# An attention and FFN block on Trainium2: the list scheduler in the source is replaced by a written order of all 2,455 operations

## The chip, the cores and the metric

One Trainium2 chip, of which the kernel uses one core. The metric is the device time of one execution in microseconds (us); before the change it is 489.09 us, the median of 3 runs (488.92 to 490.06).

The engines are called as the profile calls them: PE multiplies (TensorE), DVE is VectorE, ACT ScalarE, POOL GpSimd, and SP issues transfers. Each engine works through its own list of instructions in order; semaphores hold an instruction back until what it reads is there and what it overwrites has been read.

## The reference

```python
S, D, H, Dh, F = 2048, 512, 32, 16, 1792
xn  = layernorm(x)                                    # x [S, D], float32
q, k, v = split(xn @ wqkv)                            # 32 heads of 16
phi(u) = [softmax(u @ w_phi), softmax(-(u @ w_phi))]  # per head, 32 features
kv  = phi(k)^T v ;  z = sum_s phi(k)
o   = (phi(q) kv) / (phi(q) z + 1e-6)
s   = o @ wo
g   = silu(mish(xn @ w1 + b1) @ w2)
out = x + s * g
```

## The kernel before

Every float32 product is made of three PE products of a high and a low part (names ending in `h` and `l`: ACT rounds to the high part, and DVE or POOL subtracts it from the source to get the low one). Large products are cut 2 by 2 in the manner of Strassen, seven block products instead of eight, whose sums DVE and ACT form.

The work in order of time: the head loads x and the weights, folds `w_phi` into the weights of q and k (`wqf`, `wkf`, products with `phit`) and normalizes and transposes x (`pt`, 16 token tiles `N0` to `N15`; the transposed blocks are `fh`, `fl`). Then k and v (`kx`, `ky`, `kz`, `kj`) with the sums over tokens (`kvp`), q (8 blocks, banks `qx`, `qy`, `qz`, 256 columns a product), the first FFN product (14 blocks, `fx`, `fy`, `fz`, 512 columns; its result `hd` goes to DRAM), the attention (`ph` are transposed features of q, `pn` the products with kv), the output product (`pw`, its result goes to DRAM as `so`), and last the second FFN product (`y`, 256 columns): for each of 8 token blocks T and 7 pairs b of F chunks, `act(T, b)` loads `r`, applies mish, forms three sums in `r` (two 128x128 operations and one of 128x2x128, which the trace shows as 128x256), rounds to `ah` and subtracts to `al` (128x896), and PE multiplies seven combinations with `w2`. `final` and `gate` apply silu, multiply with `sr` (a load of `so`), add `xx` (a load of x) and store to out.

The functions of `block_kernel` do not emit instructions. They record operations in `Program` (from line 73): an operation is one instruction or a group (the six matmuls of one block product, for instance), with the tiles that it reads and writes. Some can go to either of two engines (`either`: DVE or POOL; `copy` and `held`: ACT or DVE). At the end `issue` (line 397) emits all of them at line 404, which is why most instructions of the trace have that one line; they are told apart by tiles.

What order they are emitted in is decided by `Program.order` (183) and `simulate` (222). The functions are called in the order of the string `ORDER` (parts such as `Ka2`, `Q4`, `G16`), and PE's operations keep this order. For everything else `simulate` is a list scheduler: it steps through a modelled time with the costs of `cost`, models of transfers and of the port that DVE and POOL share, and at each step gives an idle engine the ready operation whose due time (`late`) is first, if its tile buffers are free (`fits`) and nothing more urgent comes within its duration (`better`). The due time of an operation comes from the planned time of PE's next use, with single corrections from the table `SHIFT`. For an operation that two engines can take, whichever is idle first takes it.

`issue` also adds one kind of dependency: a POOL operation waits for the last DVE operation that takes the shared port, if that ends in the modelled time less than `NEAR` = 4000 ns earlier.

Tile buffers come from pools of fixed size (38 large and 15 half-size buffers, 8 PSUM banks among others); a buffer's next user waits for its last reader.

Of the kernel before, what the change touches and what calls it, by code (L numbers as in the profile page):

```python
# [48 lines left out]
SHIFT = """  # L49
kd:0:-9100 wv1:0:-1100 N1:2:-15000 N1:3:300 N1:5:5800 N1:13:4300 N1:14:-7000 kl:3:-10000 Ka2:3:-9700 N5:6:-2200  # L50
N5:8:-1200 N5:11:13000 N2:0:-3500 N2:2:-2000 N3:4:1500 N3:13:-11400 Kc0:7:4900 Kc0:10:14200 k4:0:-6900 Kd0:6:300
N6:14:-6700 P0:1:4800 P0:5:3800 P0:11:5000 Kb1:3:300 N7:6:-2800 N7:8:7300 N7:9:-6400 N8:8:-2700 N9:13:3600 Kc1:8:1800
Kd1:4:-7300 N10:3:-300 N11:0:5800 P4:0:-7000 P4:4:300 P4:5:3100 N14:8:-6800 Kd3:1:-5000 Kd3:6:-6400 A2:0:-3600
N13:5:-2500 Fa4:1:-1100 Fa4:3:3600 N15:4:10800 N15:6:-5000 N15:11:-300 Kc5:6:4400 Ka6:1:-600 Kc6:5:-300 Kc6:6:2600
P6:6:-1100 P6:8:5100 P3:3:-2600 P3:11:-2000 Kb7:1:2800 Fa3:1:-300 Fa3:3:300 P2:4:-2000 P2:6:1100 P2:10:800 Kd6:6:-8800
Kd6:9:-9500 Fb6:3:-2300 Fc3:1:1600 Fc3:2:800 Fc3:4:7900 wQ:1:2300 wQ:13:6600 Fa2:3:300 Fa2:4:-1900 Fa1:3:900
M4:1:-1400 P5:10:3200 Q0:7:14700 Q0:23:-2000 z:4:1200 z:5:11100 D0:0:800 D0:4:4700 D0:8:-800 L:5:-4200 L:9:-3000
D1:2:-8100 Q1:16:800 Q1:19:300 Q2:3:-15000 Q2:9:-2500 Q2:15:300 Q2:25:-1900 Q3:17:-4300 Q3:18:4700 Fc5:5:9400
D3:7:1800 D4:3:-4000 D4:4:6800 D4:5:1300 D4:6:11900 D4:10:11500 D5:1:-300 Fb11:1:-4700 Q4:7:-600 Q4:16:600 Q4:18:7800
Q4:20:800 Q4:21:-1400 Q4:23:-8800 Q5:25:-600 M3:1:-5000 M3:2:-6700 Fa12:1:800 D6:6:-500 D6:10:300 Fb10:1:-500  # L60
D7:1:5000 D7:4:6600 D8:1:-2400 D8:4:-500 D8:10:1400 Q6:1:4700 D9:10:800 Q7:1:7800 Q7:16:-4700 Q7:20:4800 Q7:21:-13000
Q7:23:-12900 M2:2:-5000 D10:6:-800 M6:2:-4100 D11:1:-1700 Ua0:1:-1100 Ua0:12:-800 Fc9:1:3400 D12:5:-5000 D13:0:-4400
D13:4:12500 Fa13:4:800 Ub0:14:-4300 wo0:1:-4500 Fc13:4:-13100 Fc7:2:15000 R0:8:4700 D14:6:-7800 O3:2:-900 Ua1:2:-4200
Ua1:4:-6700 Ua1:6:-3100 Ua1:11:-5000 Ua1:13:-300 Ua1:14:300 O5:2:-500 Fd13:2:-4200 O6:1:-2200 Ub1:5:-5000 Ub1:6:-2000
Ub1:8:-4500 G7:4:-2000 R2:0:-2200 R1:1:15000 R1:6:4200 R1:10:5800 G8:3:-5000 G8:6:1900 O11:2:-2000 R6:1:4900 R3:2:1600
R3:8:-3300 R4:1:2000 G11:0:-6800 G12:5:3100 G12:6:-1200 G13:5:-1100 G32:3:6500 G34:6:4000 G1:4:-15000 G3:0:5000
G4:0:-4100 G5:5:4000 G35:3:9300 G35:4:-5800 G35:6:3100 G14:0:-10200 G14:3:4000 E0:6:-2600 G15:2:800 G39:6:-300
G16:4:-5000 G41:3:1700 E5:4:-300 G20:0:800 G20:2:-2000 G20:3:-5300 G20:6:-5000 G42:3:5100 G42:5:-300 G43:2:4200
G44:2:300 G44:4:-2000 H4:2:1300 G46:3:6600 G46:6:300 G24:6:500 G47:5:-3000 G26:4:-1600 E6:2:-800 G49:0:-5000
G49:2:4000 G49:6:-1100 G49:9:2000 G49:12:-2200 G49:19:2200 G49:26:5000 G49:31:800 G49:36:2800 G49:42:-4700 G49:43:800  # L70
E7:9:-300 E7:10:15000 H3:7:2300 H6:8:800
"""
ACT_SET = {AF.Exp: 1, AF.Silu: 3, AF.Mish: 2}


class Op:
    __slots__ = ("impl", "reads", "writes", "at", "idx", "succ", "ndep", "late", "new", "ready", "start", "eng", "sets", "slack", "open", "soon", "pos", "deps", "lock", "part", "half", "code", "tiles", "shift")


class Program:  # L80


    def __init__(self, nc):
        self.eng = {"PE": nc.tensor, "V": nc.vector, "G": nc.gpsimd, "A": nc.scalar, "Q": nc.sync}
# [3 lines left out]
        self.shifts = {k: int(v) for k, _, v in (c.rpartition(":") for c in SHIFT.split())}

    @staticmethod  # L90
    def cost(e, m, a, k):
        aps = [v for v in a if isinstance(v, bass.AP)]
        n = aps[0].free_size()
        if e == "PE":
            if m == "transpose":
                return 109
            n, c = aps[2].free_size(), aps[1].free_size()
            if aps[1].dtype == F32R:
                return max(n / 2.4 + 0.104 * c, c * 0.835 + 2)
            full = 2 * max(n / 1.2 + 2.5, c * 0.835)  # L100
            if aps[1].shape[0] == 32:
                return max(0.155 * n, 24)
            return max(full * aps[0].shape[0] / P, 27)
        if e == "Q":
            return 450
# [1134 lines left out]
```

## Time and profile before

| | |
|---|---|
| time, median of 3 runs | 489.09 us (488.92 to 490.06) |
| the profiled execution, span from the first to the last instruction | 488.7 us (no other time is given for it) |
| its granted TensorE clock | 1.000 |
| PE busy | 480.2 us, 98% |
| DVE busy | 446.2 us, 91% |
| ACT busy | 293.4 us, 60% |
| POOL busy | 267.2 us, 55% |
| PE waiting after its first product | 2.8 us in 7 waits |

The span is 0.4 us below the median of the runs. A busy PE is not PE at its peak: its matmuls are pipelined, so the duration of one is longer than the interval at which they follow each other (a dense 512-column matmul has 0.39 us and follows the one before after 0.23).

In a row of a timeline the bracket holds the idle time of the engine just before the instruction and what ended it; "x6" is a run of six such instructions, whose duration is that of the run. Rows that group by form leave buffer numbers out.

### The profile page before, as it was taken

Reading aid. Unit: us, or ns where it says so; the run is one execution under the profiler, and the core shown is the slowest. Engines: PE = TensorE matmul, PEld = TensorE weight load, DVE = VectorE, ACT = ScalarE, POOL = GpSimd, SP = SyncE. Lnnn points to the kernel's source line nnn. Section 1 sums busy time; section 2 is a strip of 40 time slices with the busy share of each in tenths; the row PEclk is TensorE's granted clock in tenths of the full one; section 3 lists DMA queues with packets and bytes.
Section 4 is the critical chain, followed back from the end, with each engine's and each line's share of the span. In section 5 each row is a group of like instructions: output and inputs, shape, how many; then the busy total and the mean of one; then the engine's idle time right before and its main releaser. Section 6 shows DMA issues by size and latency. Waiting matters only on the chain.

```text
span 488.7 us, 10325 instructions
## 1 busy us (share of the span) xinstructions
PE 480.2 (98%) x3820; PEld 426.2 (87%) x3820; DVE 446.2 (91%) x893; ACT 293.4 (60%) x453; POOL 267.2 (55%) x197
## 2 busy tenths in 40 slices
PE   8899999999999999999999999999999999999996
PEld 7788888888887889898887878788899999999996
DVE  6999999988899999999999899889989889999894
ACT  3997545654556453635345545677879687777631
POOL 3989998998490446798987686370021024120030
PEclk9999999999999999999999999999999999999999
DMA  8812923968867689982959635726465646578172
GB/s 294 265 48 109 332 99 122 312 197 272 315 217 313 225 301 345 394 300 87 310 199 341 229 115 211 261 85 207 141 193 165 201 154 211 194 234 269 44 250 94
DMA packets 68641, 105.70 MB, mean 216 GB/s; under 512 B 6896, under 2 KB 37744, under 8 KB 68592
## 3 DMA queue, kind: packets, MB, share of 16 engines
q1 hardware_dynamic: 68448, 104.79, 62.9%
q8 instruction: 30, 0.49, 0.4%
q10 hardware_dynamic: 144, 0.26, 0.2%
q14 instruction: 19, 0.16, 0.1%
HBM read 60.60 MB, written 44.43 MB: 215 GB/s over the span
## 4 chain that ended last, share of the span: by engine, by line
PE 81%; DVE 8%; DMA 5%; issue 2%; ACT 1%; SPq 1%; POOL 1%; DVEq 0%; ACTq 0%
PE y L404 20%; PE fx L404 14%; PE pw L404 9%; PE kx L404 7%; PE fy L404 7%; PE qx L404 5%; PE ky L404 3%; PE fz L404 3%; PE qy L404 2%; PE kj L404 2%; PE pn L404 2%; PE kz L404 2%; DVE al L404 2%; DMA wvr<-wv 1%; DMA w1a<-w 1%
## 5 line engine op out<-in xcount | busy, mean ns | idle before, releaser
L404 POOL TENSOR_TENSOR al<-r,ah 128x896 fp32r<-128x896 f32 x8 | 17.0, 2130 | 87.4 <-DMA r<-hd 35.1
L404 ACT ACTIVATE ah<-r 128x896 fp32r<-128x896 f32 x56 | 50.9, 944 | 16.0 <-DVE r L404 12.9
L404 DVE TENSOR_TENSOR al<-r,ah 128x896 fp32r<-128x896 f32 x48 | 54.8, 1171 | 5.0 <-ACT ah L404 3.2
L404 DVE TENSOR_TENSOR r<-r 128x128 f32<-128x128 f32 (+1 forms) x157 | 48.3, 353 | 5.0 <-ACT r L404 3.4
L404 PE MATMUL y<-w2h,al 128*128 128x256 f32 x160 | 45.4, 283 | 0.0
L404 PE MATMUL y<-w2h,ah 128*128 128x256 f32 x160 | 45.3, 283 | 0.0
L404 PE MATMUL y<-w2l,ah 128*128 128x256 f32 x160 | 45.3, 283 | 0.0
L404 PE MATMUL y<-w2t,ah 128*128 128x256 f32 x224 | 41.0, 283 | 0.0
L404 PE MATMUL fx<-fh,w1b 128*128 128x512 f32 x112 | 38.8, 393 | 0.0
L404 ACT ACTIVATE r<-r 128x512 f32<-128x512 f32 x56 | 33.2, 621 | 7.9 <-DMA r<-hd 7.9
L404 PEld LDWEIGHTS y<-w2t,ah 128*128 128x128 f32 x224 | 34.9, 192 | 0.0
L404 PE MATMUL y<-w2t,al 128*128 128x256 f32 x112 | 31.7, 283 | 0.0
L404 PEld LDWEIGHTS y<-w2h,al 128*128 128x128 f32 x160 | 30.7, 192 | 0.6 <-issue 0.4
L404 PEld LDWEIGHTS y<-w2l,ah 128*128 128x128 f32 x160 | 30.7, 192 | 0.2
L404 PEld LDWEIGHTS y<-w2h,ah 128*128 128x128 f32 x160 | 30.7, 192 | 0.0
L404 PE MATMUL y<-w2g,ah 128*128 128x256 f32 x160 | 30.4, 283 | 0.0
L404 PEld LDWEIGHTS fx<-fh,w1b 128*128 128x128 f32 x112 | 21.0, 188 | 5.4 <-issue 1.2
L404 PEld LDWEIGHTS y<-w2g,ah 128*128 128x128 f32 x160 | 25.0, 192 | 0.0
L404 POOL TENSOR_TENSOR r<-r 128x128 f32<-128x128 f32 (+1 forms) x11 | 6.4, 592 | 32.3 <-DMA sr<-so 22.5
L404 PE MATMUL y<-w2g,al 128*128 128x256 f32 x80 | 22.6, 283 | 0.0
L404 ACT ACT_TABLE_LOAD x13 | 16.7, 1283 | 9.2 <-DMA x<-x 4.1
L404 PE MATMUL fx<-fl,w1b 128*128 128x512 f32 x56 | 21.8, 390 | 0.0
(766 smaller groups left out, 1730.0 us busy)
## 6 DMA issues: line engine op xcount, KB each, us to landing
r<-hd SPq DMA_DIRECT2D x56, 256.0 KB, 3.5
xd<-xc SPq DMA_DIRECT2D x8, 896.0 KB, 4.1
w1b<-w1d SPq DMA_DIRECT2D x14, 512.0 KB, 5.5
w1b<-w1d SPq DMA_DIRECT2D x14, 384.0 KB, 4.9
so<-so SPq DMA_DIRECT2D x16, 256.0 KB, 2.1
x<-x SPq DMA_DIRECT2D x15, 256.0 KB, 3.7
w1a<-w SPq DMA_DIRECT2D x7, 512.0 KB, 4.6
...
```

The costliest lines, as they stand in the source:

```text
L404: ins = getattr(e, m)(*a, **k)
```

## The change

`simulate` and all that serves it alone (the constants `PEN` to `BEGIN`, `SLACK`, `AHEAD`, `LAT`, `SHIFT`, `ACT_SET`, `cost`, `records`, `halves`, `links`, `volume`, `reads`, `bcast`, and the calls of `halves`) go. In their place stands `PLAN`, a string of 2,455 names: `Ka2.0` is the first operation that part `Ka2` records, and a last letter V, G or A gives the engine of an operation that two engines can take. `order` puts the operations in that order. Now PE's operations stand in an order of their own too, no longer in that of `ORDER`. What is computed, in which groups and with which tiles, is as before. `NEAR` is now counted in places of the plan.

```diff
-WAKE, EACH, NEAR = 15, 2, 4000
+WAKE, EACH, NEAR = 15, 2, 24
...
-SHIFT = """
-kd:0:-9100 wv1:0:-1100 N1:2:-15000 N1:3:300 N1:5:5800 N1:13:4300 N1:14:-7000 kl:3:-10000 Ka2:3:-9700 N5:6:-2200
...
+PLAN = """
+@.0 @.1 @.2 @.3 @.4 N1.0 N4.0 @.15 N4.3 @.17 N0.0 N1.1 N1.2 wv0.0 N1.3 N4.1 N4.2 @.16G N1.4 @.5 @.6 @.7 @.8 @.9 @.10
...
     def order(self):
+        at = {o.name: o for o in self.ops}
+        plan = []
+        for c in PLAN.split():
+            e = c[-1] if c[-1] in self.eng else ""
+            o = at.pop(c[:-1] if e else c)
+            o.eng = e or next(iter(o.impl))
+            plan.append(o)
+        assert not at
...
+        return plan
...
     def issue(self, tc):
         first, held = True, None
-        for o in self.order():
-            for i, (m, a, k) in enumerate(o.impl[o.eng][1]):
+        for n, o in enumerate(self.order()):
+            for i, (m, a, k) in enumerate(o.impl[o.eng]):
...
-                if i == 0 and o.eng == "G" and held is not None and o.start - held[1] < NEAR:
+                if i == 0 and o.eng == "G" and m != "dma_start" and held is not None and n - held[1] < NEAR:
...
-                held = ins.ins.name, o.start + o.impl["V"][0]
+                held = ins.ins.name, n
```

Between the first and the second left-out piece of `order` the new code also checks that the writers and readers of each tile keep the order in which the functions recorded them.

Three places of the lists of instructions. The first is PE in the head, before (the end of the first kz product, the folds `wqf` of the first pair of q weights, and the next k product `kj00`):

```order
L404 MATMUL kz2_188<-wv1l_161,fh10_105 128x512
L404 MATMUL kz2_188<-wv1h_160,fh10_105 128x512
L404 MATMUL wqf21_192<-phit_101,wqT10_190 128x128 x4
L404 MATMUL wqf31_193<-phit_101,wqT10_190 128x128 x4
L404 MATMUL kj00_194<-wv0h_142,fl00_104 128x512
L404 MATMUL kj00_194<-wv0l_143,fh00_103 128x512
L404 MATMUL kj00_194<-wv0h_142,fh00_103 128x512
L404 MATMUL kj00_194<-wv0h_142,fl00_104 128x512
L404 MATMUL kj00_194<-wv0l_143,fh00_103 128x512
```

and now, first around `wqf21`:

```order
L256 MATMUL kx2_187<-wv0l_143,fh00_103 128x512
L256 MATMUL kx2_187<-wv0h_142,fh00_103 128x512
L256 MATMUL wqf21_192<-phit_101,wqT10_190 128x128 x4
L256 MATMUL kz2_188<-wv1h_160,fl10_106 128x512
L256 MATMUL kz2_188<-wv1l_161,fh10_105 128x512
```

Behind these rows follow four more of `kz2`, the twelve of `kj00` and six of a later k product, `kj03`. The last three of those, and what now stands behind them:

```order
L256 MATMUL kj03_215<-wkh0_144,xl0_176 128x512
L256 MATMUL kj03_215<-wkl0_145,xh0_175 128x512
L256 MATMUL kj03_215<-wkh0_144,xh0_175 128x512
L256 MATMUL wqf31_193<-phit_101,wqT10_190 128x128 x4
L256 MATMUL pt2_207<-ident_83,x2_202 128x128 x4
```

`wqf31` stood directly behind `wqf21`; now 24 matmuls stand between them, and `wqf21` stands ahead of kz instead of behind it. The transposes of tile 5 (`pt5`), not shown, have moved from behind the last `wkf` fold to two folds earlier.

The second is PE in q block 4, whose last product into bank `qx4` reads `wq1`; before (the end of a product into `qx4`, one into `qy4`, and the start of the next into `qx4`):

```order
L404 MATMUL qx4_661<-wqs1h_493,fh51_589 128x256
L404 MATMUL qy4_663<-wqs1h_493,fl21_584 128x256
L404 MATMUL qy4_663<-wqs1l_494,fh21_583 128x256
L404 MATMUL qy4_663<-wqs1h_493,fh21_583 128x256
L404 MATMUL qy4_663<-wqs1h_493,fl21_584 128x256
L404 MATMUL qy4_663<-wqs1l_494,fh21_583 128x256
L404 MATMUL qy4_663<-wqs1h_493,fh21_583 128x256
L404 MATMUL qx4_661<-wq1h_489,fl61_592 128x256
L404 MATMUL qx4_661<-wq1l_490,fh61_591 128x256
```

and now (`qx4` returns after a product into `fx11`, whose first matmul stands just ahead of these rows, behind the end of the product into `qx4` with `wqs0`, and one into `fz11`):

```order
L256 MATMUL fx11_638<-fl41_588,w1b24_574 128x512
L256 MATMUL fx11_638<-fh41_587,w1b24_574 128x512
L256 MATMUL fx11_638<-fh41_587,w1b34_575 128x512
L256 MATMUL fx11_638<-fl41_588,w1b24_574 128x512
L256 MATMUL fx11_638<-fh41_587,w1b24_574 128x512
L256 MATMUL fz11_639<-fh11_581,w1b14_573 128x512
L256 MATMUL fz11_639<-fl11_582,w1b04_572 128x512
L256 MATMUL fz11_639<-fh11_581,w1b04_572 128x512
L256 MATMUL fz11_639<-fh11_581,w1b14_573 128x512
L256 MATMUL fz11_639<-fl11_582,w1b04_572 128x512
L256 MATMUL fz11_639<-fh11_581,w1b04_572 128x512
L256 MATMUL qx4_661<-wqs1h_493,fl51_590 128x256
```

Before, in all 8 q blocks, one other q product stood between a bank's products; now FFN1 products or products of other q blocks do, two at the least.

The third is POOL among the y products (`r` is loaded and summed, `al` the low parts of `act`), before:

```order
L404 TENSOR_TENSOR al4_3_996<-r4_3_994,ah4_3_995 128x896
L404 TENSOR_TENSOR al0_3_993<-r0_3_991,ah0_3_992 128x896
L404 TENSOR_TENSOR r2_5_1036<-r2_5_1036 128x128
L404 TENSOR_TENSOR r5_0_1039<-r5_0_1039 128x128
L404 TENSOR_TENSOR r2_5_1036<-r2_5_1036 128x128
L404 TENSOR_TENSOR r5_0_1039<-r5_0_1039 128x128
L404 TENSOR_TENSOR al2_6_1054<-r2_6_1052,ah2_6_1053 128x896
L404 TENSOR_TENSOR al5_4_1066<-r5_4_1064,ah5_4_1065 128x896
L404 TENSOR_TENSOR r3_0_1076<-r3_0_1076 128x2x128
L404 TENSOR_TENSOR al5_5_1069<-r5_5_1067,ah5_5_1068 128x896
```

and now, at about the same place:

```order
L256 TENSOR_TENSOR r4_5_1009<-r4_5_1009 128x128
L256 TENSOR_TENSOR r2_0_1012<-r2_0_1012 128x128
L256 TENSOR_TENSOR r0_6_1006<-r0_6_1006 128x128
L256 TENSOR_TENSOR r2_2_1027<-r2_2_1027 128x2x128
L256 TENSOR_TENSOR r2_2_1027<-r2_2_1027 128x128
L256 TENSOR_TENSOR r5_2_1058<-r5_2_1058 128x2x128
L256 TENSOR_TENSOR r2_6_1052<-r2_6_1052 128x128
L256 TENSOR_TENSOR r2_5_1036<-r2_5_1036 128x128
L256 TENSOR_TENSOR r5_2_1058<-r5_2_1058 128x128
L256 TENSOR_TENSOR r5_1_1055<-r5_1_1055 128x128
L256 TENSOR_TENSOR r3_0_1076<-r3_0_1076 128x128
L256 TENSOR_TENSOR al5_4_1066<-r5_4_1064,ah5_4_1065 128x896
```

Of the 8 subtractions `al` that POOL had, 2 are left; the others are on DVE now, and additions of `r` come to POOL from DVE. In all, the list of DVE goes from 895 to 877 rows, that of POOL from 202 to 221; 6 `al`, 6 scalings of features of k and q, 2 low parts of weights, the low part of `zacc` and one of x go from POOL to DVE, 21 `r` of 128x128 and 5 of 128x2x128 (net) from DVE to POOL. SP's transfers are the same 312 rows in another order; near the end the load of `sr13_1`, which stood behind the store of `xx9`, now stands ahead of all of the last ten stores.

## Rows read from the trace of the kernel before

**Rows 1.** The page, part 1: busy us (share of the span) and instructions of each engine.

```profile
PE 480.2 (98%) x3820; PEld 426.2 (87%) x3820; DVE 446.2 (91%) x893; ACT 293.4 (60%) x453; POOL 267.2 (55%) x197
```

**Rows 2.** The waits of PE: engine, line, waited for: us in total, times, longest.

```profile
PE wkf L404 <- DMA wkT<-wqkT: 1.0, 2, 0.7
PE wqf L404 <- ACT wqf L404: 0.7, 1, 0.7
PE pt L404 <- DVE x L404: 0.6, 2, 0.4
PE fx L404 <- DVE w1al L404: 0.3, 1, 0.3
PE kz L404 <- POOL wv1l L404: 0.2, 1, 0.2
```

**Rows 3.** Busy time: stretch, length, PE, PEld, DVE, ACT, POOL, clock, DMA share, GB/s.

```profile
20.00:140.00 120.00, 120.00 (x799) 99.73 (x799) 109.84 (x210) 76.12 (x120) 106.01 (x78) 1.00 0.59 201
160.00:484.00 324.00, 324.00 (x2596) 296.03 (x2594) 299.69 (x611) 192.94 (x295) 142.93 (x99) 1.00 0.64 215
...
4.10:467.00 462.90, 460.13 (x3667) 406.33 (x3667) 432.16 (x864) 288.18 (x445) 263.43 (x186) 1.00 0.64 219
```

**Rows 4.** PE's timeline in the head: start, us, engine, line, op [idle before <-releaser].

```profile
14.02 0.48 PE L404 MATMUL kx<-wv0h,fl 128*128 128x512 f32 x1
14.33 0.40 PE L404 MATMUL kx<-wv0l,fh 128*128 128x512 f32 x1
14.56 0.39 PE L404 MATMUL kx<-wv0h,fh 128*128 128x512 f32 x1
...
19.06 1.16 PE L404 MATMUL wqf<-phit,wqT 128*128 128x128 f32 x8 [0.69 <-ACT wqf L404]
```

**Rows 5.** PE's groups by form, q products: count | busy us, mean ns | idle before.

```profile
L404 PE MATMUL qx<-wq1h,fl 128*128 128x256 f32 x16 | 5.4, 334 | 0.0
...
L404 PE MATMUL qx<-wqs0h,fl 128*128 128x256 f32 x16 | 4.9, 304 | 0.0
...
L404 PE MATMUL qx<-wqh,fl 128*128 128x256 f32 x16 | 4.5, 281 | 0.0
```

**Rows 6.** DVE's groups by form.

```profile
L404 DVE TENSOR_TENSOR al<-r,ah 128x896 fp32r<-128x896 f32 x48 | 54.8, 1171 | 5.0 <-ACT ah L404 3.2 <-POOL al L404 1.6
L404 DVE TENSOR_TENSOR r<-r 128x128 f32<-128x128 f32 x106 | 30.0, 315 | 1.5 <-POOL r L404 0.9
...
L404 DVE TENSOR_TENSOR w1sl<-w1s,w1sh 128x1024 fp32r<-128x1024 f32 x6 | 7.3, 1222 | 0.0
```

**Rows 7.** POOL's groups by form.

```profile
L404 POOL TENSOR_TENSOR al<-r,ah 128x896 fp32r<-128x896 f32 x8 | 17.0, 2130 | 87.4 <-DMA r<-hd 35.1 <-DVE al L404 27.8 <-ACT ah L404 23.9
...
L404 POOL TENSOR_TENSOR r<-r 128x128 f32<-128x128 f32 x6 | 2.7, 467 | 22.5 <-DMA sr<-so 22.5
```

**Rows 8.** DVE's timeline at 459 us.

```profile
459.06 5.09 DVE L404 TENSOR_TENSOR al<-r,ah 128x896 fp32r<-128x896 f32 x5
```

**Rows 9.** PE's timeline at 467 us.

```profile
467.05 0.28 PE L404 MATMUL y<-w2h,al 128*128 128x256 f32 x1
```

**Rows 10.** The timelines of DVE and ACT in the tail, in order of time.

```profile
480.99 0.43 DVE L404 TENSOR_TENSOR yc<-yc,sr 128x256 f32<-128x256 f32 x1 [3.17 <-DMA sr<-so]
...
484.27 0.36 ACT L404 ACTIVATE u<-y 128x256 f32<-128x256 f32 x1
...
485.19 0.42 DVE L404 TENSOR_TENSOR u<-u,sr 128x256 f32<-128x256 f32 x1
485.65 0.42 DVE L404 TENSOR_TENSOR xx<-u,xx 128x256 f32<-128x256 f32 x1
```

**Rows 11.** The timelines of POOL and DVE near 470 us, in order of time.

```profile
469.09 1.30 POOL L404 TENSOR_TENSOR sr<-yy,sr 128x512 f32<-128x512 f32 x1 [0.50 <-ACT yy L404]
469.47 1.48 DVE L404 TENSOR_TENSOR sr<-yy,sr 128x512 f32<-128x512 f32 x1
...
472.07 0.68 DVE L404 TENSOR_TENSOR sr<-yy,sr 128x512 f32<-128x512 f32 x1
```

More of the change, by code (lines that the diff above doesn't have):

```diff
@@ L1 @@
 from contextlib import ExitStack, contextmanager
-import heapq
 import numpy as np
@@ L55 @@
[L55 to L59, printed above, removed]
@@ L72 @@
+E7.27 E7.28 E7.29 E7.30
 """
-ACT_SET = {AF.Exp: 1, AF.Silu: 3, AF.Mish: 2}
 class Op:
-    __slots__ = ("impl", "reads", "writes", "at", "idx", "succ", "ndep", "late", "new", "ready", "start", "eng", "sets", "slack", "open", "soon", "pos", "deps", "lock", "part", "half", "code", "tiles", "shift")
+    __slots__ = ("impl", "reads", "writes", "idx", "name", "eng", "lock")
 class Program:
@@ L84, in __init__ @@
         self.eng = {"PE": nc.tensor, "V": nc.vector, "G": nc.gpsimd, "A": nc.scalar, "Q": nc.sync}
-        self.ops, self.tag, self.cap, self.pe = [], {}, {}, []
-        self.group, self.slack, self.part, self.half = None, SLACK, None, False
+        self.ops, self.tag, self.cap = [], {}, {}
+        self.group, self.part = None, None
         self.region, self.count = {}, {}
[L88 to L105, printed above, removed]
-        if e == "A":
-            return (60 if aps[1].space == "PSUM" else 110) + 0.833 * n + 93 * sum(isinstance(v, bass.AP) for v in k.values())
-        psum = any(v.space == "PSUM" for v in aps[1:])
-        nn = max(v.free_size() for v in aps)
-        if e == "V":
-            if m == "reciprocal":
-                return 70 + 6.3 * n
-            if m in ("tensor_scalar", "tensor_copy") and not psum:
-                return 70 + 0.52 * n
-            return 70 + 1.04 * nn
-        if k.get("op") == ALU.pow:
-            return 520
-        return (140 + 1.73 * n) if bcast(a) else (140 + 2.17 * n)
-    @staticmethod
-    def records(m, a, k):
-        return 2 if m == "transpose" or a[1].dtype == F32R else 4
     def names(self, v):
@@ L419, in locks @@
     return aps[0].free_size() > 1 if m in ("tensor_scalar", "tensor_copy") else len(aps) > 2
-def volume(aps):
-    runs = []
-    for v in aps[:2]:
-        n = 1
-        for st, c in reversed(list(v.ap)):
-            if st != n:
-                break
-            n *= c
-        runs.append(n)
-    return aps[0].free_size() * aps[0].shape[0] * (4 if min(runs) > 128 else 4.7)
-def reads(aps):
-    return "DRAM" not in str(aps[0].space).upper()
-def bcast(a):
-    return any(st == 0 and n > 1 for v in a if isinstance(v, bass.AP) for st, n in v.ap)
 class Engine:
```

388 lines of the change are left out of this document (140 added, 248 removed).

## The prediction

> **What bounds the kernel now.** The page's busy line comes first [rows 1]: the reader sees PE at 480.2 of 488.7 us, DVE at 446.2, ACT and POOL far below. Second, PE by stretches [rows 3]: from 20 to 140 us and from 160 to 484 us PE is busy for the whole of the stretch, so the middle of the program can be shortened only by what hides inside busy time. PE's granted clock is 1.00 in these rows, the higher level (2.4 GHz), so no clock is there to be won. Third, the waits of PE [rows 2]: they come to 2.8 us after the wake-up products, 2.5 of them before 20 us and 0.3 near 150 us. The change keeps every matmul, so a floor is near: these 2.8 us, what hides in the q products, and the tail after the last matmul. DVE stands second: it idles 462.9 − 432.2 = 30.7 us from 4.1 to 467 us [rows 3], and it delivers what PE reads. A new order can lose there much more than it can win.
>
> **Head.** Two of PE's waits have one cause each in its order. The second half of the first q fold (wqf31) stood right behind the first (wqf21), and needed a buffer that ACT had first to write: 0.69 us [rows 4]. Now 6 kz, 12 kj00 and 6 kj03 matmuls stand between them. One dense matmul follows the next after 0.23 us (14.33 to 14.56 [rows 4]), so 24 of them cover 5.5 us: the 0.7 is gone. The first kz product waited 0.2 us for POOL's wv1l [rows 2]; wqf21 now stands ahead of it and takes longer than 0.2 us: gone too. The transposes pt5 stood between the last wkf fold and the first kx; they now stand two folds earlier, while PE waits for a load anyway. That brings kx's start forward from 14.02 us by 0.1 to 0.4 us; I take 0.3. The other waits (wkf 1.0, pt 0.6) hang on loads: the same transfers stand ahead of the last wkT half on SP, so I leave them. Head: −0.7 − 0.2 − 0.3 = **−1.2**. Bounds: −2.5 if every head wait goes, 0 if loads that are exchanged on SP (wkT01 now behind the 512 KB of wvr0) cost as much as is won.
>
> **The q products.** No wait shows here, but the matmul that opens a product does: qx from wq1h takes 334 ns, from wqs0h 304, where a plain one takes 281 [rows 5]. With 16 of each that is 16 × (53 + 23) = 1.2 us. The cause I read from the order: a q block multiplies into bank qx four times, and all 32 times in the kernel that a q product goes back to a bank, just one other product of six 256-column matmuls stands between, half the columns of six 512-column ones and so some 6 × 0.115 = 0.7 us. The bank must be read out by ACT or DVE in that time. In the new order the closest return comes after two FFN1 or several q products (2.1 us or more by the same intervals), so the readout has three times as long. I take the whole **−1.2**; the bound on the other side is 0, if the readout is late for another reason.
>
> **Mixing.** Where PE goes over from transposes or folds to dense products the first one is longer: 0.48 us against 0.40 [rows 4]. The new order has 40 stretches of such kinds where the old had 36: +0.1 to +0.4; I take **+0.2**.
>
> **The tail.** DVE waited 3.17 us for a load of sr [rows 10], issued on SP behind the store of xx9, and its four last tiles then ran one behind another: the last xx starts at 485.65 and ends at 486.07. The last u leaves ACT at 484.27 + 0.36 = 484.63; with a free DVE two operations of 0.42 follow, 0.46 apart as in these rows, and end at about 485.6. The new order issues all sr and xx loads before those stores. I take **−0.45**; bounds 0 and −0.5.
>
> **DVE's load, the dear term.** The order moves 16 long subtractions from POOL to DVE (6 al of 128x896 and 10 of 128x1024) and sends some 26 short r additions the other way. At 1.171 and 1.222 us [rows 6] the long ones cost DVE 6 × 1.171 + 10 × 1.222 = 19.2 us; the short ones, 21 of 128x128 and 5 of twice the width that I count as two, spare it 31 × 0.315 = 9.8 us. With smaller moves DVE carries some 5 us more over the kernel. What matters is the load ahead of a date. I take al7_2, which ends at 459.06 + 5.09 = 464.15 [rows 8], and which PE needs at 467.05 [rows 9]. The new DVE list has 845 instead of 859 instructions ahead of it, but 52 new ones of 37.5 us against 66 gone of 29.6, by the durations of the same operations before: +7.9 us. If DVE idled as long as before, al7_2 would end at 472.05. PE, 1.2 + 1.2 − 0.2 = 2.2 us earlier, wants it at 464.85. So PE waits 7.2 us less whatever DVE's idle time falls by.
>
> How much will it fall? Much of the 30.7 us is time in which DVE was early (2.9 us at al7_2), and such idle time goes first when work is added. And DVE's instructions that read two SBUF operands were held up while POOL ran: an addition of 128x512 took 1.48 us beside POOL's of 469.09, alone 0.68 [rows 11]. Long POOL instructions of 2.13 us [rows 7] become fewer, which gives back a part of the 16 moves. I take a fall of 6.7 us, so **+0.5** for PE; bounds 0 and +7.2.
>
> The Trainium skill (SBUF — State Buffer, section "SBUF: two separate sides") says that the pair of ports that VectorE and GpSimd share is an exclusive lock, held for a whole instruction, and that the loser is fully blocked. Our row at 469.47 agrees: it ends at 470.95, 0.56 us after POOL's instruction does at 470.39, as if it had begun only then. By that rule alone the short additions are a bad trade, since each would block DVE for POOL's 0.467 us [rows 7] instead of 0.315, 31 × 0.152 = 4.7 us lost where the count above has 9.8 saved; against it the 6 al would free 6 × (2.130 − 1.171) = 5.8 us. By the rule the two nearly cancel, and PE's wait would lie near my 0.5.
>
> **The sum.** −1.2 − 1.2 + 0.2 − 0.45 + 0.5 = −2.15 against the profiled span of 488.7 us, which is 486.5. The median of the runs, 489.09, stands 0.4 above this span; I carry that over: **486.9 us**.
>
> **Rivals.** About 0.3%, 1.47 us, is what a measurement of this kernel can tell from no change: faster is below 487.6, slower above 490.6.
> (a) *DVE eats the gain.* Its idle time falls by 3.1 to 6.0 us instead of 6.7, PE waits 1.2 to 4.1 us, for w1al, ph, al or r. For it: DVE is at 91%, and PE already waits for it once, at w1al near 150 us [rows 2]; by the durations before, the new list puts 1.9 us more of work ahead of that w1al. Against it: an order without DVE's own waits for ACT could fill most of the 30.7 us. Time 487.6 to 490.6, say 489.0. Chance 0.27.
> (b) *DVE becomes the bound; slower.* One mechanism, at the y products: al comes late and each of PE's products stands behind it. It decides when DVE's idle time falls by less than 3.1 us; with none at all, PE waits 7.2 us, and the time is 489.09 − 2.65 + 7.2 = 493.6. For it: the sum of DVE's instructions rises and nothing in the list shortens them; the short additions go to an engine that holds DVE up [rows 11]. Against it: DVE was 2.9 us early. Chance 0.15.
> (c) *Nearly every wait goes*: half of the loads' 1.6 us and the 0.3 at w1al too, and no wait for DVE comes. That is −1.2 − 0.8 − 0.3 − 1.2 + 0.2 − 0.45 = −3.75, or 485.3. Against it: a load's date does not hang on PE's order. Chance 0.05.
> That the order does not do what it says can be left aside: each engine's list shows it moved, with the same matmuls. A limit that hides behind the list (a transfer that waits for a buffer) is in the ends of (a) and (b).
>
> **How the numbers follow.** Forecast 0.53, (a) 0.27, (b) 0.15, (c) 0.05. Faster: forecast and (c), 0.58; same: (a), 0.27; slower: (b), 0.15. The range runs from 485.3, case (c), to 490.6, the upper end of (a): it leaves out (b) and what lies below (c), under 2 in 10.
>
> **What would show it.** Right: PE's list of waits without wqf from ACT and kz from POOL; kx starting at 13.6 to 13.9 us; the two qx forms at about 281 ns; no wait of DVE for sr near the end; DVE idle to PE's date of al7_2 at 24 us or less. Wrong: new lines in PE's waits with DVE as the releaser and more than 1.2 us together (then (a) or (b), told apart by their sum against 4.1), at w1al, pn or y; the qx forms still at 300 ns and over, which would mean that the cause isn't the bank's return; or a later kx, which would mean that the exchanged loads cost what the transposes won.

## The result, and the profile after

The changed kernel takes **491.73 us** (median of 6 runs, 490.82 to 492.88), the kernel before 489.52 (6 runs, 488.92 to 490.78): a ratio of 1.0045, 95% interval 1.003 to 1.006. It is slower by 2.2 us, where 486.9 was forecast.

The profiled execution of the change has a span of 489.4 us and took 491.07. Its page, part 1, and the waits of PE, which answer to [rows 1] and [rows 2]:

```profile
PE 480.9 (98%) x3820; PEld 426.0 (87%) x3820; DVE 446.2 (91%) x875; ACT 287.8 (59%) x452; POOL 263.4 (54%) x216
```

```profile
PE y L256 <- DVE al L256: 1.3, 4, 0.4
PE wake L256 <- DVE mhalf L358: 1.1, 1, 1.1
PE wkf L256 <- DMA wkT<-wqkT: 0.8, 1, 0.8
PE fy L256 <- DVE ol L256: 0.5, 2, 0.3
PE pt L256 <- DVE rs L256: 0.2, 1, 0.2
```

The waits for wqf and kz are gone, as forecast; new ones for DVE stand in y and in late FFN1. DVE's busy time is to the tenth what it was, 446.2 us.

**The span before was no fair base.** In later runs of the kernel before, time and span differ by 1.9 us (490.11 us with a span of 488.2, 488.64 with 486.7), so its profiled span of 488.7 belongs to an execution of about 490.6 us (an estimate). The experiment e1 below runs the old order in the new code in 489.5 us, and its traced lists are those of the kernel before, row for row on every engine; its profile has a span of 487.3, with kx at 13.09 us instead of 14.02 [rows 4] and no wait for kz. I compare the change with e1: the spans differ by 2.1 us, the medians by 2.2.

From the starts in PE's timeline I took, for each matmul from the first kx to the last y, the interval to the next, less that of a dense one of its size (0.227 us at 512 columns, 0.120 at 256, 0.104 for a fold, 0.021 for pn), and summed by product. "Attention" is FFN1 behind 255 us (late FFN1) with pn and pw:

| us lost by PE in | e1 | change | difference |
|---|---|---|---|
| k and FFN1 up to 255 us | 2.65 | 2.76 | +0.1 |
| folds wqf | 1.11 | −0.01 | −1.1 |
| q | 1.25 | −0.12 | −1.4 |
| attention | 0.90 | 2.93 | +2.0 |
| y | 0.11 | 3.14 | +3.0 |

From the last y matmul's start (482.30 and 484.94 us) to the end of the last xx (484.66 and 486.57) is 2.36 us in e1, 1.63 now, −0.7; from there to the end of the span it is 0.2 more. The sum is 0.1 − 1.1 − 1.4 + 2.0 + 3.0 − 0.7 + 0.2 = +2.1.

PE's timeline in the head of the change answers to [rows 4]: neither fold waits now. Its groups by form answer to [rows 5]: a q product that returns to a bank costs what a plain one does.

```profile
13.05 0.48 PE L256 MATMUL kx<-wv0h,fl 128*128 128x512 f32 x1
...
14.53 1.05 PE L256 MATMUL wqf<-phit,wqT 128*128 128x128 f32 x8
...
20.91 1.05 PE L256 MATMUL wqf<-phit,wqT 128*128 128x128 f32 x8
```

```profile
L256 PE MATMUL qx<-wqs0h,fl 128*128 128x256 f32 x16 | 4.5, 282 | 0.0
L256 PE MATMUL qx<-wq1h,fl 128*128 128x256 f32 x16 | 4.5, 281 | 0.0
```

In the tail DVE's last two rows of the change stand 0.46 us apart, as they did before; but DVE no longer waits for sr, and it is free (0.30 us idle) when ACT's last u comes, which answers to [rows 10]:

```profile
485.68 0.43 DVE L256 TENSOR_TENSOR u<-u,sr 128x256 f32<-128x256 f32 x1 [0.30 <-ACT u L256]
486.14 0.43 DVE L256 TENSOR_TENSOR xx<-u,xx 128x256 f32<-128x256 f32 x1
```

Now the y products, where it loses most, and one of the waits there. The timelines of ACT, DVE and PE in the change, each in order of time:

```profile
353.41 0.95 ACT L256 ACTIVATE ah<-r 128x896 fp32r<-128x896 f32 x1
356.03 0.63 ACT L256 ACTIVATE r<-r 128x512 f32<-128x512 f32 x1 [1.67 <-DMA r<-hd]
356.57 0.94 ACT L256 ACTIVATE ah<-r 128x896 fp32r<-128x896 f32 x1
```

```profile
354.40 1.09 DVE L256 TENSOR_TENSOR al<-r,ah 128x896 fp32r<-128x896 f32 x1 [1.79 <-ACT ah L256]
357.54 1.09 DVE L256 TENSOR_TENSOR al<-r,ah 128x896 fp32r<-128x896 f32 x1 [2.05 <-ACT ah L256]
```

```profile
358.04 0.28 PE L256 MATMUL y<-w2h,ah 128*128 128x256 f32 x1
358.69 0.39 PE L256 MATMUL y<-w2t,al 128*128 128x256 f32 x1 [0.37 <-DVE al L256]
```

PE waits for al1_6, and DVE was not busy then: it stood idle for 2.05 us, waiting for ah1_6. ACT had that ready to do, but ahead of it in ACT's list stands mish of r4_5, whose load landed at 356.0 and which PE needs only near 389 us. This place costs 0.5 us. At three others of 0.3 to 0.6 us (388.7, 448.9 and 467.6 us) DVE itself works without a gap on rows that are needed later and stand ahead of the al. Matching each al's end with PE's first row that reads it, e1's order leaves 3 to 19 us between them, most of them 8 to 16; the new one leaves 0 to 9, about 3 in the middle. ACT waits longer for loads of r than in e1, where it was 6.3 us in 3 waits:

```profile
ACT r L256 <- DMA r<-hd: 15.7, 13, 1.8
```

### The profile page after: what moved, and what is told of

Same layout as the page of the kernel before. It is cut to its first block, busy times and chain, and to the rows that moved or that the text cites. A ratio compares the mean times of both kernels' runs of the same rounds, so it can differ in the third digit from the quotient of the medians.

```text
span 489.4 us, 10262 instructions
## 1 busy us (share of the span) xinstructions
PE 480.9 (98%) x3820; PEld 426.0 (87%) x3820; DVE 446.2 (91%) x875; ACT 287.8 (59%) x452; POOL 263.4 (54%) x216
## 5 line engine op out<-in xcount | busy, mean ns | idle before, releaser
L256 POOL TENSOR_TENSOR r<-r 128x128 f32<-128x128 f32 (+1 forms) x37 | 23.0, 635 | 84.9 <-DVE al L256 19.2
L256 DVE TENSOR_TENSOR al<-r,ah 128x896 fp32r<-128x896 f32 x54 | 58.4, 1092 | 9.2 <-ACT ah L256 9.0
L256 DVE TENSOR_TENSOR r<-r 128x128 f32<-128x128 f32 (+1 forms) x131 | 43.4, 365 | 6.2 <-ACT r L256 3.8
L256 PE MATMUL y<-w2t,ah 128*128 128x256 f32 x224 | 42.6, 283 | 0.0
L256 PE MATMUL y<-w2g,ah 128*128 128x256 f32 x160 | 31.4, 283 | 0.0
L256 ACT ACTIVATE hc<-fy,b1t 128x512 f32<-128x512 f32 x14 | 9.4, 689 | 23.5 <-PE fy L256 17.7
L256 PEld LDWEIGHTS y<-w2t,al 128*128 128x128 f32 x112 | 21.5, 192 | 1.1 <-DVE al L256 1.1
L256 POOL TENSOR_TENSOR sr<-yy,sr 128x512 f32<-128x512 f32 x3 | 4.4, 1464 | 32.8 <-DVE xx L256 29.0
```

Of the source, the lines that this page charges most:

```text
L256: ins = getattr(e, m)(*a, **k)
```

## The experiments

In the diffs A is the list of names of the change and B that of the order before (places and engines as its scheduler chose them); a line with three names shows a moved operation between its neighbours. In each, PE's losses are counted as in the table above. The intervals are of the ratio to the kernel before on the same chip.

**e1, the old order in the new code.**

```diff
-@.0 @.1 @.2 @.3 @.4 N1.0 N4.0 @.15
+N1.0 @.0 @.1 N4.0 @.2 @.3 N4.3 @.4
...
```

> The old order, written out as a plan and issued by the new code, so that only the rule for POOL's port dependency differs (24 places instead of 4000 ns). Theory 1 (the loss of the change lies in the order of the second FFN product): same as before within 0.3%, span about 488.5 us. Rival 2 (the loss comes from the port dependency counted in places): slower than before by 1 to 3 us, with POOL and DVE waiting for each other more. The run also gives the old order's span beside its own time, which is missing so far: the changed kernel's runs take 1.7 us more than their spans.

Measured: 489.50 us, 1.0004 (0.9995 to 1.0013). The order is the whole of the change; counting `NEAR` in places costs nothing that this interval can show.

**e2, e3, e4: parts of either order.** The cuts lie at the first pn and at the first y product of PE.

```diff
-PLAN = A
+e2: A up to Ua0.0 (pn), the other names as in B
+e3: B up to the first y, the other names as in A
+e4: A up to the first y, the other names as in B
```

> The new order up to the first attention product pn, the old order for everything behind it. Theory 1: the gains of the head and of the q products (about 1.6 + 1.2 us) stay and no wait for al comes, so 2 to 3 us less than before, 486.5 to 487.5 us. Rival 3 (the new order hands over a late DVE: 4.8 us more DVE work is done by 311 us): the old order behind it starts late and loses the gain, 489 us or more, with PE waiting for DVE after 262 us.

> The old order up to the first product of the second FFN (y), the new order behind it. Theory 1: no gain at the front, and the waits for al in the y products with 3 us as in the changed kernel, and its later tail: 492 to 493 us, slower than both. Rival 3: with an early DVE handed over, the y products of the new order run without waits for al: 489 us or less.

> The new order up to the first y product, the old order for the y products and the tail. Theory 1: the gains of head and q stay, the three waits for bank readouts between 275 and 293 us (1.2 us) are in it, no waits for al: about 1.4 us less than before, 487.5 to 488.5 us, 1 us above the kernel that has the new order only up to pn. Rival 3: 490 us or more.

Measured: e2 491.39 us, 1.0040 (1.0026 to 1.0053); e3 494.28, 1.0113 (1.0092 to 1.0133); e4 489.26, 0.9999 (0.9990 to 1.0008). With e1 and the change, e3 and e4 make a square: the new y part costs 2.5 us behind the new front (491.73 − 489.26) and 4.8 behind the old one. The new front gains 0.2 us in front of the old y part (489.50 − 489.26) and 2.55 in front of the new one (494.28 − 491.73). The 0.2 is so little, though e4 has no loss in wqf and q, because it loses 2.9 us in the attention and 1.1 in y, at the joint of the two orders near 320 us. In e2, whose attention is the old one, one wait stands at 271 us in the profiled execution, one of its longer ones (492.76 us); the row of PE's waits, and the windows behind it (columns as in [rows 3]):

```profile
PE fx L254 <- ACT hd L254: 3.0, 1, 3.0
```

```profile
270.00:274.00 4.00, 1.16 (x6) 0.61 (x4) 4.00 (x12) 0.86 (x3) 2.35 (x1) 0.93 0.93 340
274.00:278.00 4.00, 3.85 (x9) 3.08 (x10) 2.43 (x13) 1.56 (x5) 2.62 (x2) 0.50 0.65 252
278.00:282.00 4.00, 4.00 (x14) 3.13 (x14) 2.85 (x8) 1.61 (x6) 2.18 (x2) 0.72 0.12 46
282.00:286.00 4.00, 4.00 (x49) 2.97 (x48) 2.99 (x6) 3.06 (x7) 2.22 (x2) 1.00 0.24 88
```

The readout hd stood in ACT's list behind one (oh) that had to wait for POOL. Behind the wait PE's granted clock is 0.50 and 0.72, so the wait costs about twice its length: late FFN1 loses 6.7 us in this execution.

**e5, e6, e7: single places, and the engines.** e5 moves two operations of the attention, e6 seven in y (three are shown), e7 gives 77 operations of the y part the engine, DVE or POOL, that they had before, at the new places.

```diff
-e5: Fa7.2 wo0.2G Q7.18
+e5: Fc10.5 wo0.2G Q7.17G
-e5: D14.3 Ub0.8 D11.10
+e5: Ub0.7 Ub0.8 Fd8.2
-e6: G29.6V G33.1 G13.5
+e6: G13.5 G33.1 G13.6V
-e6: G14.6V G33.6V G18.4V
+e6: G14.5 G33.6V G14.6V
-e6: G49.41V G49.20V E3.2
+e6: G49.40 G49.20V G49.41V
-e7: R0.2V ... R1.1G ... G7.2V
+e7: R0.2G ... R1.1V ... G7.2G
```

> The changed kernel with two operations moved in the attention part: on POOL the low part wo0l ahead of the second subtraction of q15e (it frees the buffer that ol00 needs), on DVE the second ol11 ahead of two reductions (tz14, tz13) of 1.2 us each. Theory 1 (single operations stand in a list behind others that are late or not yet due, and a PSUM bank comes free too late): the waits of PE at 275.8, 277.7 and 292.5 us go, 0.46 + 0.41 + 0.29 us and some 0.1 us for each restart, so 1.2 to 1.5 us less than the changed kernel, 490.2 to 490.5 us. Rival 3 (DVE has too much work ahead of it): the waits only move to the next bank, less than 0.5 us gained.

> The changed kernel with seven operations moved in the second FFN product, no engine changed: on ACT the mish of r4_5 (whose load lands late, needed 30 us later) behind ah1_6; on DVE al4_5 ahead of al2_0, an addition of yy4 ahead of three sums, the last sum of r6_2, its ah and its al ahead of two sr and xx operations, and al7_2 ahead of al7_5. Theory 1: the waits at 358.0, 388.7, 411.9, 448.9 and 467.6 us go (0.53 + 0.50 + 0.21 + 0.58 + 0.33 = 2.1 us and about 0.1 for each restart), so 2 to 2.7 us less than the changed kernel, 489 to 489.7 us. Rival 3: DVE's load stays the same, so the waits move to other al, and less than 0.7 us is gained.

> The changed kernel with the engines of before for 77 operations of the second FFN product and its weights that DVE or POOL can take (so 6 al and others back on POOL, sums of r back on DVE), places unchanged. Rival 4 (the exchange between DVE and POOL makes al late): most of the 3 us of waits go, 489 us or less. Theory 1: the places were chosen for these engines, POOL's al of 2.1 us come later still, and the time gets no shorter than 491 us, rather 492 to 495.

Measured: e5 492.43 us, 1.0058 (1.0042 to 1.0073); e6 490.73, 1.0032 (1.0018 to 1.0045); e7 499.46, 1.0204 (1.0189 to 1.0219). e5 missed: wo0l, now ahead of the second subtraction of q15e in POOL's list, started at 270.57 us and took 2.4, so that subtraction came at 272.94 instead of 270.35; and ACT, with the exp of q15e next in its list, did not read out the bank that PE wanted:

```profile
PE y L254 <- DVE al L254: 2.8, 3, 1.7
PE fx L254 <- ACT ha L254: 1.5, 1, 1.5
```

e6 gained 1.0 us, about half of what I expected (y loses 2.4 us instead of 3.1); the wait at 358 us is gone, the one at 448.9 stays (0.5), and near 366 us PE loses 0.6 where the change loses 0.3. e7 is the worst of all: y loses 9.0 us. Its waits of PE in y:

```profile
PE y L254 <- DVE yy L254: 2.5, 4, 1.2
PE y L254 <- DVE al L254: 2.4, 3, 1.2
...
PE y L254 <- POOL al L254: 0.5, 1, 0.5
```

So the exchange of engines alone is not what makes the new y part slow: taking it back at the new places makes it worse. That places and engines were fitted to each other is my reading; the new engines at the old places were not run.

**e8 and e9: the new front, mended, with the old y part.** e8 is e4 with the moves of e5 and six readouts oh and ol at the joint earlier; e9 is e4 with the reduction q15r later, ol11 earlier and four of those readouts moved.

```diff
-e8: R2.5 Ua1.11 G9.4V
+e8: O6.1A Ua1.11 Ua1.13
-e9: Ua0.2 Q7.19 Ua0.5
+e9: Ua0.8 Q7.19 Fb13.1A
-e9: D14.3 Ub0.8 D11.10
+e9: Ub0.7 Ub0.8 Fd8.2
```

> The new order up to the first y product with the two moves of the attention part, the old order behind it, and at the joint the last six oh and ol operations ahead of a rounding of w2 on ACT. Theory 1: from the 489.3 us of the kernel without these moves go 1.2 us at 275 to 293 us, the two waits of y for ol at 320 us (0.9 us), and some 0.4 us of restarts: 486.6 to 487.2 us, faster than both kernels. If it stays at 489 us, another engine behind PE has become the limit in the y part.

> The new order up to the first y product, the old one behind it (489.3 us as it stood), with six operations moved: on DVE the reduction of q15r (1.2 us) behind the second ol10 and the second ol11 ahead of the reductions tz14 and tz13; at the joint two oh ahead of a rounding of w2 on ACT and two ol ahead of a sum of r on DVE. POOL's list is left alone, since moving wo0l there made the features of q15 late and PE wait 1.7 us. Theory 1 (a bank is freed late because single operations that nobody waits for stand ahead of it): the waits at 275 to 293 us (1.2 us) and at 320 us (0.9 us) go with their restarts, 487 to 487.6 us, faster than both kernels. Rival 3 (DVE has too much work there): the waits come back at other banks and the time stays at 489 us or more.

Measured: e8 492.34 us, 1.0055 (1.0035 to 1.0075); e9 489.53, 1.0006 (0.9997 to 1.0015). In e9 late FFN1 and pw lose 1.2 us less than in e4, pn 1.0 more and y 0.3 more: the waits moved. e8 repeats e5's wait and has one of 1.9 us at the joint; windows behind that:

```profile
324.00:328.00 4.00, 2.10 (x13) 1.58 (x11) 2.16 (x7) 2.96 (x9) 3.65 (x3) 1.00 0.18 68
328.00:333.00 5.00, 5.00 (x17) 3.96 (x16) 5.00 (x7) 1.80 (x4) 2.37 (x1) 0.66 0.11 41
333.00:338.00 5.00, 5.00 (x29) 4.37 (x28) 5.00 (x14) 3.66 (x6) 0.00 (x0) 1.00 0.19 68
```

**e10 and e11: fifteen moves in the new order, two in the old.** e10 is the change with e9's two moves in the attention, e6's seven and six more of their kind in y (a mish or sum that is needed late goes behind an ah or al that is needed soon). These are thirteen moves in y; the expectation of e13 counts them as eleven. e11 is e1 with the second wqf fold behind kj00, and the last loads of sr and x ahead of the stores.

```diff
-e10: G15.0 G3.1 G29.7
+e10: G0.5 G3.1 G2.1
-e10: G15.1 G0.6V E1.1
+e10: E1.0A G0.6V G2.3G
-e11: N5.7 wq1.3 N2.6
+e11: Ka0.1 wq1.3 wq1.4A
-e11: G49.52 E7.6 E7.5 G49.53
+e11: G49.51 E7.6 E7.5 H1.9
```

> The changed kernel with the two moves of the attention part as in the run above, the seven moves in the y part of the earlier run (which gave 1.0 us), and four more there: the mish of r4_4 behind ah4_2 and those of r0_3 and r0_2 behind ah0_0 on ACT, with al4_2 and al0_0 ahead of sums of r0_2 on DVE, and al6_2 ahead of sums of r7_0. Theory 1: from 490.7 us go the waits at 365, 366 and 449 us (1.2 us, restarts 0.3) and, where the y part does not take it back, the 1.2 us of the attention part: 488 to 489.3 us. Rival 3: the y part takes back what the front gains, 490 us or more.

> The old order with two of the terms of the forecast alone: the second half of the first q fold (wqf31) behind the twelve kj00 products, and the loads of sr13_1 and xx13_1 on SP ahead of the stores of xx4, xx11 and xx9. Both terms hold as forecast: PE's wait for wqf of 0.7 us goes (a restart of 0.1 more), DVE's wait of 3 us for sr near the end goes and the last xx ends 0.45 to 0.75 us earlier behind the last y product: 488.0 to 488.6 us. Rival: the wait of 0.7 comes back at the next fold or PE catches up on a load that lands no earlier, and the tail is bound by its last stores: 489.2 us or more.

Measured: e10 489.80 us, 1.0015 (1.0005 to 1.0026), 1.9 less than the change, or 1.5 by the two ratios, each on its own chip; y loses 1.1 us instead of 3.1, and no wait for al is left among PE's:

```profile
PE wake L254 <- DVE mhalf L356: 1.1, 1, 1.1
PE wqf L254 <- DMA wqT<-wqkT: 0.7, 1, 0.7
PE pt L254 <- ACT x L254: 0.4, 1, 0.4
PE pn L254 <- DVE ha L254: 0.2, 1, 0.2
PE pt L254 <- DVE rs L254: 0.2, 1, 0.2
```

Fifteen places out of 2,455, with the same engines and the same work for DVE, take back two thirds of what y lost. The time between al's end and PE's first read is still short (0.1 to 9 us, 2.3 in the middle); gone are the places where an al was late by half a microsecond. e11: 490.33 us, 1.0026 (1.0016 to 1.0037), a miss. Its tail took 1.62 us instead of 2.36, but the fold's wait did not go: kj now waits 0.7 us for wqf, and 0.8 for v besides. So the gain at wqf needs more than that one place.

**e12 and e13: DVE relieved ahead of the attention.** Open was why every version with the new front gives its 2.4 us back in the attention. With the new order DVE is busy longer up to 262 us, and it transposes ph from q8e later; the windows and the row in e1, and in the change:

```profile
4.10:262.00 257.90, 256.48 (x1823) 219.82 (x1823) 244.35 (x470) 146.33 (x234) 200.62 (x140) 1.00 0.71 246
4.10:467.00 462.90, 461.48 (x3680) 408.33 (x3680) 433.30 (x865) 288.80 (x445) 264.15 (x187) 1.00 0.64 219
...
268.14 0.71 DVE L253 STREAM_TRANSPOSE ph<-q8e 128x512 f32<-128x512 f32 x1
```

```profile
4.10:262.00 257.90, 256.83 (x1848) 220.45 (x1859) 247.37 (x474) 141.94 (x232) 190.90 (x137) 1.00 0.71 242
4.10:467.00 462.90, 459.88 (x3662) 405.32 (x3661) 431.37 (x843) 281.85 (x442) 255.31 (x202) 1.00 0.65 218
...
271.91 0.70 DVE L256 STREAM_TRANSPOSE ph<-q8e 128x512 f32<-128x512 f32 x1
```

e12 is e4, e13 the change with e10's moves in y alone; in both, six bank readouts go from DVE back to ACT, at their places:

```diff
-Kb5.3V ... Kb6.1V ... Fb3.1V ... Q2.7V ... Q3.7V ... Q4.5V
+Kb5.3A ... Kb6.1A ... Fb3.1A ... Q2.7A ... Q3.7A ... Q4.5A
```

> The new order up to the first y product, the old one behind it (as e4), with six bank readouts of the front (three 128x512, three 128x256) given back from DVE to ACT, their places unchanged: 3 x 0.69 + 3 x 0.42 = 3.3 us less for DVE. Theory D (DVE's load ahead of the attention is what takes the front's gain back: in 4.1 to 262 us it is busy 247.4 us with the new order and 244.4 with the old, its idle time falls from 13.6 to 10.5): the long first scalings of DVE in the attention come 1.5 to 3 us earlier, PE's losses in late FFN1, pn, pw and at the joint fall by 1.5 to 2.5 us in sum, time 487.0 to 488.0. Theory P (the places of the rows in the attention are the cause, DVE's load is not): losses as in e4, 489.0 to 489.6. Theory A (ACT reads the banks out too late, since these rows now queue behind its exps): slower than e4, above 489.8, with PE waits for ACT in the k or q products.

> The change with the eleven moves in the y part of e10 and the same six readouts on ACT; the attention's rows stand where the change put them. Theory D: y loses about 1.1 us as in e10 and the attention 1.5 to 2.5 less than in the change: 487.5 to 488.8. Theory P: only the y part is better than in the change, 489.4 to 490.0.

Measured: e12 489.61 us, 1.0011 (1.0001 to 1.0021); e13 489.98, 1.0019 (1.0008 to 1.0030). The time is theory P's, not D's. The window and the row in e12:

```profile
4.10:262.00 257.90, 256.81 (x1832) 220.28 (x1831) 244.60 (x467) 144.53 (x238) 190.74 (x137) 1.00 0.71 242
...
272.17 0.70 DVE L254 STREAM_TRANSPOSE ph<-q8e 128x512 f32<-128x512 f32 x1
```

DVE has 2.8 us less to do up to 262 us, as in e1, and the transposes come no earlier: it only idles more. The attention loses 2.88 us (e4: 2.91). But this does not clear DVE's load as a whole. The six readouts stood at 86 to 205 us. From there to the first of these transposes DVE is almost never idle; the windows of e1, the change, e12 and e16 (below):

```profile
205.00:268.14 63.14, 63.14 (x471) 54.80 (x470) 60.21 (x122) 26.83 (x42) 51.75 (x32) 1.00 0.74 250
205.00:271.91 66.91, 66.91 (x473) 57.19 (x472) 65.43 (x135) 27.92 (x45) 54.37 (x35) 1.00 0.72 239
205.00:272.17 67.17, 67.09 (x472) 57.03 (x472) 65.24 (x134) 28.33 (x46) 54.40 (x35) 1.00 0.71 239
205.00:270.23 65.23, 65.15 (x464) 55.45 (x463) 62.99 (x124) 28.07 (x45) 53.88 (x34) 1.00 0.69 232
```

In this stretch the change gives DVE 5.2 us more work than e1 and leaves it 1.5 us of idle time instead of 2.9; the transposes come 3.8 us later. e12 took almost nothing away there. So e12 excludes the load ahead of 205 us, and the load behind it stays as a rival that no run took away by itself.

**e14 to e18: one wait after the other.** e14 is e2 with its wait's cause taken away, e12's readouts on ACT and e11's earlier loads. Each that follows keeps the moves of the one before.

```diff
-e14: wo0.2G Ua0.1 D9.9
+e14: Fa13.1A Ua0.1 D12.2
-e14: Fc9.3 Fc9.1 Q7.17G
+e14: Fc8.4 Fc9.1 Q7.25
-e15: Fd8.2 Fc9.4 Q7.19
+e15: D12.3 Fc9.4 D8.8V
-e16: Q7.23G D12.0G Fd8.0
+e16: D8.6 D12.0G Fc8.1
-e17: Fa7.2 Fa13.3 Fa7.1A
+e17: Ua0.1 Fa13.3 D12.2
-e17: Fd8.2 Q7.19 Fa13.0
+e17: Ua0.16 Q7.19 Fb7.2
-e18: Fb7.3A D13.0V R1.0
+e18: Ub0.14 D13.0V D12.10
```

> The new order up to the first pn product, the old one behind it (as e2), with the cause of e2's 3.0 us wait taken away: on ACT the readout oh of pn now stands behind the readouts of fx9 and fx13, on DVE hc ahead of a reduction and hb ahead of another; the six readouts of e12 on ACT, and the last load of sr and of x issued ahead of the stores (as in e11). If the places at the joint were all that held e2 back, the front's gain of 2.4 us and the tail's 0.7 both show: 486.4 to 487.8, clock 1.000. If DVE, which in e2 reached the attention 2.3 us later than in the old order, is late for ol as well, PE waits 1 to 3 us more for ol: 488.5 to 490.5.

> e14 with one operation moved: hb9, the readout of bank fy9 on DVE, for which PE waited 2.0 us at 271 us in e14, now stands ahead of the two scalings q8e and q9e. If places decide, and not DVE's load, that wait goes whole and little comes back behind it: e14's median of 489.74 less 1.5 to 2.2, so 487.5 to 488.3. If DVE's chain through the attention is the limit (it has no gap from 264 to 281 us in e14), the wait comes back as waits for ol or pn at 276 to 282 us: 489.2 to 489.8.

> e15 with two more: POOL forms ez12 ahead of the two rows of q14e and of DVE's hc8 and ha9, so that DVE's idle 1.96 us in front of the reduction tz12 goes, and DVE's reduction q14r stands behind that of tz10. If DVE's chain is the limit, this brings all of the attention 1 to 2 us forward and gains that over e15; if e15 has already no loss in the attention, the two are the same within 0.3 us.

> e16 with two operations moved on DVE: ha13, the readout of bank fz13 for which PE waited 1.35 us at 276 us, stands ahead of the sums den, and the reduction q15r stands behind the last readout ol of the first pn products. If the places of single readouts are all that is left, the 1.5 us go and the front's gain shows: 487.4 to 488.0, the kernel faster than before. If a row behind it is late in its turn (ol for pn at 279 us, or pw at 288 us), a part comes back: 488.0 to 489.0.

> e17 with one more move: the row ez13 on DVE (2.2 us) stands behind the readouts ol01 instead of ahead of them, so that these come 2.2 us earlier and the wait of pw for ol (0.45 us lost in e16) goes. Same as e17 or up to 0.6 us faster: 487.0 to 488.0; if ez13's own followers are late then, slower than e17, with a wait of PE for ph or ol between 295 and 320 us.

| | time, us | ratio, interval | attention | y | PE's largest wait there |
|---|---|---|---|---|---|
| e14 | 489.74 | 1.0012 (1.0003 to 1.0020) | 4.16 | 0.06 | fx for hb, 2.0 |
| e15 | 490.30 | 1.0025 (1.0016 to 1.0033) | 4.42 | 0.06 | fy for ha, 2.4 |
| e16 | 489.04 | 0.9992 (0.9983 to 1.0001) | 3.44 | 0.06 | fy for ha, 1.3 |
| e17 | 489.43 | 1.0004 (0.9995 to 1.0012) | 3.49 | 0.06 | pn for ol, 0.6 |
| e18 | 490.23 | 1.0024 (1.0015 to 1.0033) | 4.67 | 0.06 | pw for ol, 1.5 |

All of them keep the gain in wqf and q, and with the old y part none loses anything there. In the attention most of a removed wait comes back behind it, at a later row of DVE's list. The rows of e16 (its wait, and DVE's work in front of it) and of e17:

```profile
PE fy L254 <- DVE ha L254: 1.3, 1, 1.3
...
270.23 0.70 DVE L254 STREAM_TRANSPOSE ph<-q8e 128x512 f32<-128x512 f32 x1
...
274.96 0.35 DVE L254 TENSOR_TENSOR ol<-pn,oh 128x256 fp32r<-128x256 f32 x1
275.24 0.67 DVE L254 TENSOR_TENSOR ha<-ha,fz 128x512 f32<-128x512 f32 x1
```

```profile
PE pn L254 <- DVE ol L254: 0.6, 1, 0.6
PE pw L254 <- DVE ol L254: 0.4, 1, 0.4
```

e16, where POOL's ez12 stands earlier and a reduction of DVE later, moved the chain itself: the transposes come at 270.23 us, after 272.43 in e15 and 271.91 in the change, with 2.4 us less work for DVE from 205 us on than in the change, and it has the lowest ratio of all. It can't be told from the kernel before; no version beat that one.

## Why the prediction was wrong

- **wqf, −0.7: right in kind, it was −1.1.** The fold's wait is gone.
- **kz −0.2 and kx −0.3: not there.** Both rested on rows of an execution whose head ran late. The old order in e1 has no wait for kz and starts kx at 13.09 us, the new one at 13.05. From the same execution came the base: I added 0.4 to go from its span to the median, where the span belonged to a run 1.5 us above the median. A right base makes the sum's answer about 488 (489.5 − 2.15, and the 0.5 of kz and kx not there), not 486.9; it would still be wrong.
- **q, −1.2: right, −1.4.** The qx forms went to 281 and 282 ns, and in no run with the new q order did they cost more than a plain one. The cause read from the order, the early return to a bank, agrees with every run, but no run changed the return alone.
- **Mixing, +0.2:** nothing of its own was measured; k and early FFN1 together changed by 0.1.
- **Tail, −0.45: right in sign, −0.7**, past the bound of −0.5. e11 has it from the two moved loads alone; but e2, e4 and e12, where these loads stand behind the stores as before, have a tail of 1.68 us as well, since sr landed there 3.9 to 4.2 us ahead of the last y matmul (e2, e4) and not 2.8 (e1). So what counts is how far ahead of PE's end the load lands, and a later PE gives that too.
- **The failing step is the dear term, DVE +0.5** ("a fall of 6.7 us", bounds 0 and +7.2). PE's loss to late deliveries rose by 3.0 in y and 2.0 in the attention, inside my outer bounds but for another reason than the term has. The step summed DVE's work ahead of one date, al7_2, and asked how much of its idle time the work would fill. (Of its 16 "subtractions" six are scalings and one an addition; the durations hold.) Up to 467 us DVE's idle time did not fall: 29.6 us in e1 (462.9 − 433.3), 31.5 in the change, where the sign of being right was 24 or less. The added work did not come either: DVE is busy 431.4 us instead of 433.3, in part because one al now takes 1.092 us instead of 1.171 [rows 6]; the group in the change:

```profile
L256 DVE TENSOR_TENSOR al<-r,ah 128x896 fp32r<-128x896 f32 x54 | 58.4, 1092 | 9.2 <-ACT ah L256 9.0
```

  So by 467 us DVE has 2 us less to do and is late all the same: at 357 us it waits for ah, ACT for a load, and at 388.7 us it works on al2_0, needed later, ahead of al4_5. The error was to price a new order by the sum of an engine's work and its idle time over the whole program and for one date near its end. What sets a delivery in lists that are worked in order is what stands directly ahead of it on each engine that it passes through. e10 (thirteen places in y, the same engines, two thirds of y's loss back) shows that for y. In the attention, a date that the term left out, the sum does fit when it is taken from 205 us on: 5.2 us more work for DVE than in e1, 1.5 less idle, 3.8 later. That is read from the traces; e16 agrees with it, and no run took work away there by itself.
- **The rivals:** (b) named one place, the y products behind a late al, and the sign, but not the mechanism, for DVE was no bound there: from the first y product to the last it is busy 143.4 of 166.0 us, in e1 146.8 of 163.0. (a) named ph, where the attention's loss begins; its time did not come, nor did (c). The sign that was to tell (a) from (b) fails: PE's waits for DVE come to 1.8 us in the list, (a)'s side of 4.1, while the starts show 5.0 and the time lies above 490.6.
- **The rule of the Trainium skill** that I weighed (SBUF — State Buffer, section "SBUF: two separate sides") gave near zero for the exchange of long and short instructions; DVE's shorter al agrees with it in sign. It bears on durations, and durations were not what failed.
- **What I left out:** that a gain on PE in front of the attention needs DVE's chain there to start earlier too. PE starts its last q matmul 2.4 us earlier (251.83 and 249.42 us), DVE's transposes of ph came 3.8 later.

**What stays open:** whether some order starts DVE's chain in the attention as much earlier as PE now ends q. e12 excludes DVE's load ahead of 205 us as what holds it. Behind that DVE works almost without a gap, and its load there is the likeliest bound. In e16 the transposes came 2.2 us earlier than in e15, with ez12 from POOL earlier and one reduction later; the two, and the rest of DVE's rows there, weren't separated.

## What to carry to other kernels

Judge a written order by its margins: for each tile that the busiest engine reads, the time between its end and that first read, and what stands ahead of it in the list of every engine it passes through; work that is needed 30 us later and waits for a load must not stand ahead of work that is needed at once. Busy sums and idle sums over the whole program say nothing of that; over the stretch in front of one date, behind the engine's last long idle time, they can. Before you carry a gain to the end, follow it to the next stage that another engine feeds, and take the base from more than one execution: here the same order's spans differ by more than 1 us.
